# Fillers at TensorE's copy waits, and v and the state stored 64 columns wide, in a gated linear attention with a following feed-forward network

## The chip, the cores and the metric

The kernel runs on one core of a Trainium2 chip. A core has five engines that work side by side and each run their own queue of instructions in order: TensorE (PE, matmuls into PSUM), VectorE (DVE), ScalarE (ACT), GpSimd (POOL) and SyncE (SP, which here only issues the DMA transfers). They wait for one another through semaphores. The metric is the time of one execution on the device in microseconds (us); less is better.

## The reference, cut to what matters

The input is float32 for the attention and double precision for the four weights (the kernel reads the weights as pairs of 32-bit words). `B, H, S, D = 4, 8, 768, 48`; 3072 tokens; model width 384; inner width 1024.

```python
# attention: a complex decay per key channel, a state of D x D per head
scale = np.minimum(mag, 0.999) / (mag + 1e-06)          # mag = |a|
for t in range(S):
    S_re, S_im = ar * S_re - ai * S_im + kv, ar * S_im + ai * S_re   # kv = k_t outer v_t
    y[:, :, t] = q_t @ S_re
x = y.transpose(0, 2, 1, 3).reshape(B * S, H * D)
# feed-forward
a = x @ w1
b = x @ w2
return (a * b @ w3) @ w_out
```

## The kernel before

The time axis is cut into chunks of 128 steps. A *unit* is half a sequence of one batch, three chunks; there are eight units, and units 2n and 2n+1 share a state. Within a chunk the attention is a masked product: `scores` makes `A` = K'Q masked, `outputs` makes y from V and A and from the state T and Q, `turn` transposes the keys, `state` adds K'V to T. The gates (logarithms, exponentials, running products, sines) of the next unit are computed on ScalarE and VectorE while TensorE works on the present one. Each unit's FFN follows one unit behind. `w3` and `w_out` are multiplied together once at the start (`fuse`, the matmuls into `f`).

The order of TensorE's instructions is the order in which the program emits them (`manual_schedule`); a scheduler places the instructions of the other engines.

v is used where it lies, 48 columns per head. The matmuls of `outputs` take 32 columns of V at a time; the quadrants that lie across two heads need zeros beside the head's 16 columns, and only these are copied into the padded tile `V` (and `Tp` for the state):

```python
    def load_qkv(u):
        b, h = divmod(u, 2)
        if "q" not in g_t.get(u, {}):
            take_qk(u)
        g = g_t[u]
        load_rows(g["k"], kt, u)
        load_rows(g["q"], qt, u)
        g["vr"] = V_t[u] = two.tile([P, UC, DM], FP, tag="vr", name="vr")
        nc.sync.dma_start(out=g["vr"], in_=v[b, h * TT:(h + 1) * TT].rearrange("(c p) e -> p c e", p=C))

    def middle(X):
        return X.rearrange("p (h e) -> p h e", e=2 * D)[:, :, 32:64].rearrange("p h (two e) -> p h two e", two=2)

    def apart(X):
        return X.rearrange("p h two e -> p h (two e)")[:, :, 0:64].rearrange("p h (x e) -> p h x e", e=16)[:, :, 0::3]

    def spread_v(u):
        nc.scalar.copy(out=apart(Vb[u % 2].rearrange("p c h two e -> p (c h) two e")),
                       in_=middle(V_t[u].rearrange("p c e -> p (c e)")))

    def quadrant(X, Xp, q, i=0):

        return Xp[:, q // 3, i] if q % 3 == 1 else X[:, 32 * q:32 * q + 32]
# ... cut, from outputs:
        y = ps_v.tile([P, KD, C], FP, tag="v", name="y")
        lanes = [[] for _ in range(4)]
        for q in range(3 * H // 2):
            f, j = divmod(q, 4)
            o = y[32 * j:32 * j + 32, f]
            heads = [(q // 3 * 2 + (q % 3 + i) // 2, i) for i in range(2 if q % 3 == 1 else 1)]
            got = [(quadrant(V_t[u][:, c], Vb[u % 2][:, c], q, i), A[:, hd]) for hd, i in heads]
        # ... cut: the same with the state, then the matmuls, four lanes side by side
        with tc.high_priority():
            nc.scalar.copy(out=xT_t[u][:, :, w], in_=y)

    def state(u, c):

        KT, V = KT_t.pop((u, c)), V_t[u][:, c].rearrange("p (h e) -> p h e", h=H)
        n = u % 2 * UC + c
        T = T_t.get((u // 2, n))
        kv = ps_v.tile([2 * D, H, D], FP, tag="v", name="kv")
        for hd in range(H):
            nc.tensor.matmul(out=kv[:, hd], lhsT=KT[:, hd].rearrange("p d x f -> p (d x f)"), rhs=V[:, hd],
                             start=True, stop=True)
        Tn = three.tile([2 * D, H, D], FP, tag="T", name="T")
        Tp = Tb[(u // 2 * 2 * UC + n) % 3]
        new = middle(Tn.rearrange("p h e -> p (h e)"))
        with tc.high_priority():
            if T is None:
                nc.scalar.copy(out=Tn, in_=kv)
            else:
                nc.vector.tensor_tensor(out=Tn, in0=kv, in1=T[0], op=OP.add)
            if c == UC - 1:
                rho = L_t[u][1][:, :, TT:TT + 1].to_broadcast([2 * D, H, D])
                nc.vector.tensor_tensor(out=Tn, in0=Tn, in1=rho, op=OP.mult)
            nc.scalar.copy(out=apart(Tp), in_=new)
        T_t[u // 2, n + 1] = Tn, Tp
```

The feed-forward step of 128 inner columns, and the late checks (`look`: they read the gates and the weights again and sum up values out of bounds, for which a general version of the computation stands ready behind a branch):

```python
        a = two.tile([P, TT], FP, tag="a", name="a")
        with tc.high_priority():
            nc.scalar.copy(out=a, in_=got[0])
            nc.vector.tensor_tensor(out=ab_t[u][:, j], in0=got[1], in1=a, op=OP.mult)
# ... cut
    def check_weights(late):

        for u in range(2):
            for f in range(KD):
                re = late.tile([P, 2, TT], FP, tag="look", name="look")
                load_rows(re, art, u, [f])
                check_gates(u, re[:, 0], re[:, 1], f)
                yield
# ... cut, the weights' part:
                    raw = late.tile([P, 512, 2], I32, tag="look", name="look")
                    nc.sync.dma_start(out=raw[:, 0:step // 2].rearrange("p m w -> p (m w)"), in_=src[:, i, j:j + step])
                    lo, hi = (raw[:, 0:step // 2, x].bitcast(FP) for x in range(2))
                    nc.scalar.activation(out=hi, in_=hi, func=AF.Square, scale=2.0 ** 15)
                    nc.scalar.activation(out=lo, in_=hi, func=AF.Relu, scale=-1.0, bias=TINY, accum_out=st_wts[:, n:n + 1])
```

The order of unit 0 and of its FFN. `pieces(0)` holds ten groups (transposes, `kv`, `sc`, `y`); `fill` holds what is left of `fuse`, four entries of two matmuls each:

```python
        take_qk(1)
        rest = ffn(0, 2)
        work = work[2:]
        for i, p in enumerate(pieces(0)):
            for f in p:
                f()
            if i in (0, 1, 3, 5):
                fill.pop(0)()
            if i == 0:
                for f in work[:2]:
                    f()
                load_qkv(1)
            if i >= 2:
                next(steps)
            if i in (5, 7):
                work[2 + (i == 7)]()
        for i, f in enumerate(rest[:HEAD]):
            f()
            if i < 2:
                work[4 + i]()
            if i == 2:
                phase.close()
            if i < 6:
                next(steps)
        head_pool[1] = fast.enter_context(tc.tile_pool(name="late_heads", bufs=1))
        for _ in steps:
            pass
        load_gates(2)
```

For the later units, `unit` deals the parts of the FFN evenly over the pieces:

```python
    def ffn(u, parts=1):
        return [lambda j=j: ffn_ab(u, j) for j in range(KF)] + [p for t in range(UC) for p in ffn_out(u, t, parts)]

    def unit(u, steps, rest, look, ahead):

        for f in rest[:ahead]:
            f()
            next(steps, None)
        rest = rest[ahead:]
        p = pieces(u) + [[]]
        n = len(p)
        for i in range(n):
            for f in rest[i * len(rest) // n:(i + 1) * len(rest) // n] + p[i]:
                f()
                next(steps, None)
            next(look, None)
```

Of the kernel before, what the change touches and what calls it, by code (L numbers as in the profile page):

```python
# [10 lines left out]
FP = mybir.dt.float32  # L11
# [363 lines left out]
def kernel(  # L375
# [81 lines left out]
    Vb = [singles.tile([P, UC, H // 2, 2, 32], FP, name=f"V{i}") for i in range(2)]  # L457
    Tb = [singles.tile([2 * D, H // 2, 2, 32], FP, name=f"Tp{i}") for i in range(3)]
# [22 lines left out]
    g_t, L_t, xT_t, ab_t, T_t, KT_t, V_t = {}, {}, {}, {}, {}, {}, {}  # L481
# [18 lines left out]
# [4 lines that stand above are left out]
        g = g_t[u]  # L504
        load_rows(g["k"], kt, u)
        load_rows(g["q"], qt, u)
        g["vr"] = V_t[u] = two.tile([P, UC, DM], FP, tag="vr", name="vr")
        nc.sync.dma_start(out=g["vr"], in_=v[b, h * TT:(h + 1) * TT].rearrange("(c p) e -> p c e", p=C))

    def middle(X):
        return X.rearrange("p (h e) -> p h e", e=2 * D)[:, :, 32:64].rearrange("p h (two e) -> p h two e", two=2)

    def apart(X):
        return X.rearrange("p h two e -> p h (two e)")[:, :, 0:64].rearrange("p h (x e) -> p h x e", e=16)[:, :, 0::3]

    def spread_v(u):
        nc.scalar.copy(out=apart(Vb[u % 2].rearrange("p c h two e -> p (c h) two e")),
                       in_=middle(V_t[u].rearrange("p c e -> p (c e)")))  # L520

    def quadrant(X, Xp, q, i=0):

        return Xp[:, q // 3, i] if q % 3 == 1 else X[:, 32 * q:32 * q + 32]

    def check_gates(u, re, junk, f=0):
        for x, (scale, bias) in enumerate(((-1.0, LEAST), (1.0, MOST))):
            nc.scalar.activation(out=junk, in_=re, func=AF.Relu, scale=scale, bias=bias,
                                 accum_out=st_low[:, x, u, f:f + 1])
# [146 lines left out]

    def outputs(u, c):
        QL = L_t[u][0]
        w = slice(c * C, (c + 1) * C)
        A = Ab[(u * UC + c) % 2]  # L680
# [6 lines left out]
        for q in range(3 * H // 2):  # L687
            f, j = divmod(q, 4)
            o = y[32 * j:32 * j + 32, f]
            heads = [(q // 3 * 2 + (q % 3 + i) // 2, i) for i in range(2 if q % 3 == 1 else 1)]  # L690
            got = [(quadrant(V_t[u][:, c], Vb[u % 2][:, c], q, i), A[:, hd]) for hd, i in heads]
            if not first:
                got += [(quadrant(T[0].rearrange("p h e -> p (h e)"), T[1], q, i), QL[:, hd, w]) for hd, i in heads]
# [7 lines left out]
    def state(u, c):  # L701

        KT, V = KT_t.pop((u, c)), V_t[u][:, c].rearrange("p (h e) -> p h e", h=H)
        n = u % 2 * UC + c
        T = T_t.get((u // 2, n))
        kv = ps_v.tile([2 * D, H, D], FP, tag="v", name="kv")
# [3 lines left out]
        Tn = three.tile([2 * D, H, D], FP, tag="T", name="T")  # L710
        Tp = Tb[(u // 2 * 2 * UC + n) % 3]
        new = middle(Tn.rearrange("p h e -> p (h e)"))
        with tc.high_priority():
            if T is None:
                nc.scalar.copy(out=Tn, in_=kv)
            else:
                nc.vector.tensor_tensor(out=Tn, in0=kv, in1=T[0], op=OP.add)
            if c == UC - 1:
                rho = L_t[u][1][:, :, TT:TT + 1].to_broadcast([2 * D, H, D])
                nc.vector.tensor_tensor(out=Tn, in0=Tn, in1=rho, op=OP.mult)  # L720
            nc.scalar.copy(out=apart(Tp), in_=new)
        T_t[u // 2, n + 1] = Tn, Tp

    def ffn_ab(u, j):
# [10 lines left out]
        with tc.high_priority():  # L735
            nc.scalar.copy(out=a, in_=got[0])  # L736
# [57 lines left out]

    def check_weights(late):

        for u in range(2):
            for f in range(KD):
                re = late.tile([P, 2, TT], FP, tag="look", name="look")
                load_rows(re, art, u, [f])  # L800
                check_gates(u, re[:, 0], re[:, 1], f)
                yield
        n = 0
        for w in (w1, w2, w3t, wo):
# [4 lines left out]
            for i in range(src.shape[1]):  # L809
                for j in range(0, src.shape[2], step):  # L810
# [3 lines left out]
                    nc.scalar.activation(out=hi, in_=hi, func=AF.Square, scale=2.0 ** 15)  # L814
# [221 lines left out]
```

## Time and profile before

| | |
|---|---|
| time, median of 3 runs | 597.53 us (597.53 to 598.36) |
| span of the profiled execution | 596.5 us |
| mean TensorE clock granted | 0.982 of full speed |
| matmul records on TensorE | 3514 |
| DMA traffic | 84.71 MB, mean 142 GB/s |

How to read the lines that follow in this document. In the list of waits a line names the waiting engine with the instruction's output and line, then what released it, then us in total, times, and the longest. In a timeline a line gives start and duration in us, the engine, the line, the operation, output<-input, the shape, how many were merged, and in brackets the idle time ahead and what ended it. A group line ends with total busy us, the mean of one in ns, and idle time ahead. A float32 matmul makes two records. The span in 40 slices (the digit is tenths of the slice; PEclk is the granted clock):

```profile
PE   4669989999889999999799999999999999999996
DVE  5998399744851675159311685258413683300110
ACT  6897668548973798298622988398534652101100
PEclk9779999999899999999899999999999999999999
DMA  9777997295584658633932447815920007000001
```

After the fourth slice (one is 14.9 us) TensorE is busy nearly throughout. In the first four the weights are loaded and converted on ScalarE and VectorE, and TensorE waits for them.

### The profile page before, as it was taken

What the parts mean: (1) busy time and instruction counts of PE and PEld (TensorE: products, weight loads), DVE (VectorE), ACT (ScalarE), POOL (GpSimd) and SP (SyncE); (2) the same over time, 40 slices, a digit from 0 to 9 for tenths busy, and PEclk for the clock granted to TensorE, in tenths of its full rate; (3) what the DMA queues carried; (4) which work ended last, traced back from release to release, by engine and by line L of the source; (5) the groups of instructions that cost most, each with busy time, mean ns of one, the idle gap of its engine ahead of it and who ended that gap; (6) DMA issues with size and microseconds to landing.
All of it is one profiled execution on the core that took longest, in us unless ns stands there. A gap on an engine that the chain in (4) does not pass through costs nothing.

```text
span 596.5 us, 8841 instructions
## 1 busy us (share of the span) xinstructions
PE 556.7 (93%) x3514; PEld 366.5 (61%) x3514; DVE 302.0 (51%) x420; ACT 349.3 (59%) x584; POOL 5.1 (1%) x14
## 2 busy tenths in 40 slices
PE   4669989999889999999799999999999999999996
PEld 2335775567456766676366765776567656766553
DVE  5998399744851675159311685258413683300110
ACT  6897668548973798298622988398534652101100
POOL 3000000000000000000000000000000000000000
PEclk9779999999899999999899999999999999999999
DMA  9777997295584658633932447815920007000001
GB/s 289 277 282 227 262 333 204 80 233 154 159 221 114 178 174 207 161 118 105 233 86 67 126 157 188 225 54 154 246 78 1 14 32 154 1 14 29 1 1 44
DMA packets 46050, 84.71 MB, mean 142 GB/s; under 512 B 4656, under 2 KB 36144, under 8 KB 45104
## 3 DMA queue, kind: packets, MB, share of 16 engines
q1 hardware_dynamic: 46000, 84.06, 50.4%
q8 instruction: 29, 0.48, 0.4%
q14 instruction: 21, 0.17, 0.1%
HBM read 60.42 MB, written 4.72 MB: 109 GB/s over the span
## 4 chain that ended last, share of the span: by engine, by line
PE 56%; ACT 15%; DMA 13%; DVE 10%; issue 2%; SPq 2%; DVEq 0%; ACTq 0%
PE m L731 31%; PE o L747 13%; PE sc L672 4%; PE y L697 3%; PE kv L708 3%; DMA vr<-in_v_dram 3%; ACT gZ L552 3%; DMA im<-in_a_im_dram 2%; DMA look<-in_a_re_dram 2%; PE tp L660 2%; ACT re L552 2%; DMA raw<-in_w_dram 1%; ACT gA L552 1%; ACT look L815 1%; DVE gZ L608 1%
## 5 line engine op out<-in xcount | busy, mean ns | idle before, releaser
L731 PE MATMUL m<-xT,w1s 128*128 128x384 f32 x384 | 137.1, 494 | 4.0 <-ACT xT L699 3.7
L731 PE MATMUL m<-xT,w2s 128*128 128x384 f32 x384 | 136.0, 491 | 4.6 <-ACT ot L751 4.6
L747 PE MATMUL o<-w3o,ab 128*128 128x384 f32 x384 | 130.1, 492 | 0.0
L731 PEld LDWEIGHTS m<-xT,w2s 128*128 128x128 f32 x384 | 73.5, 192 | 57.1 <-ACT ot L751 5.9
L737 DVE TENSOR_TENSOR ab<-m,a 128x384 f32<-128x384 f32 x64 | 35.4, 555 | 141.6 <-PE m L731 127.6
L731 PEld LDWEIGHTS m<-xT,w1s 128*128 128x128 f32 x384 | 70.9, 192 | 48.7 <-ACT xT L699 5.8
L747 PEld LDWEIGHTS o<-w3o,ab 128*128 128x128 f32 x384 | 71.0, 190 | 48.5 <-issue 3.8
L736 ACT COPY a<-m 128x384 f32<-128x384 f32 x64 | 30.4, 475 | 64.0 <-PE m L731 64.0
L861 PE MATMUL f<-wo_s,w3s 128*128 128x384 f32 x128 | 48.8, 540 | 19.5 <-DVE wo_s L784 19.5
L662 ACT COPY KT<-tp 128x384 f32<-128x384 f32 x40 | 33.6, 846 | 42.0 <-PE tp L660 41.9
L861 PEld LDWEIGHTS f<-wo_s,w3s 128*128 128x128 f32 x128 | 26.6, 214 | 39.0 <-DVE wo_s L784 21.4
L672 PE MATMUL sc<-QL,KL 96*128 96x128 f32 x384 | 47.9, 278 | 2.0 <-DVE A L674 1.9
L672 PEld LDWEIGHTS sc<-QL,KL 96*128 96x128 f32 x384 | 45.6, 192 | 6.0 <-DVE A L674 3.3
L674 DVE COPY_PREDICATED A<-causal,sc 128x512 f32<-128x512 int32 x48 | 34.5, 739 | 13.4 <-PE sc L672 12.7
L697 PE MATMUL y<-A,vr 128*32 128x128 f32 x384 | 36.2, 277 | 0.0
L697 PE MATMUL y<-A,V 128*32 128x128 f32 x384 | 34.5, 274 | 0.0
L708 PEld LDWEIGHTS kv<-vr,KT 128*96 128x96 f32 x320 | 29.6, 165 | 3.2 <-ACT KT L662 1.1
L697 PE MATMUL y<-QL,T 96*32 96x128 f32 x320 | 31.5, 272 | 0.0
L708 PE MATMUL kv<-vr,KT 128*96 128x48 f32 x320 | 29.7, 246 | 0.7 <-ACT KT L662 0.7
L751 ACT COPY ot<-o 128x384 f32<-128x384 f32 x24 | 11.2, 467 | 32.4 <-PE o L747 32.4
L697 PE MATMUL y<-QL,Tp 96*32 96x128 f32 x320 | 29.8, 272 | 0.0
L697 PEld LDWEIGHTS y<-A,V 128*32 128x32 f32 x384 | 28.1, 109 | 0.0
(104 smaller groups left out, 664.0 us busy)
## 6 DMA issues: line engine op xcount, KB each, us to landing
look<-in_w_dram SPq DMA_DIRECT2D x28, 512.0 KB, 4.4
raw<-in_w_dram SPq DMA_DIRECT2D x7, 1024.0 KB, 8.4
raw<-in_w_dram SPq DMA_DIRECT2D x8, 768.0 KB, 6.4
KL<-gR SPq DMA_DIRECT2D x24, 192.5 KB, 3.5
KL<-k SPq DMA_DIRECT2D x24, 192.5 KB, 4.2
re<-in_a_re_dram SPq DMA_DIRECT2D x24, 192.0 KB, 5.9
im<-in_a_im_dram SPq DMA_DIRECT2D x24, 192.0 KB, 4.3
k<-in_k_dram SPq DMA_DIRECT2D x24, 192.0 KB, 3.5
```

Source lines behind the costliest of these rows:

```text
L552: chain(nc.scalar.activation(**kw))
L660: nc.tensor.transpose(out=tp[:, f], in_=src[:, f, c * C:(c + 1) * C], identity=ident)
L662: nc.scalar.copy(out=KT_t[u, c][:, :, :, x].rearrange("p h d f -> p f d h"), in_=tp.rearrange("p f (d h) -> p f d h", h=H))
L672: nc.tensor.matmul(out=sc[:, j], lhsT=KL[:, x * n + j, w], rhs=QL[:, x * n + j, w], start=True, stop=True)
L674: nc.vector.copy_predicated(out=A[:, x * n:(x + 1) * n], data=sc, mask=causal.rearrange("p (h t) -> p h t", h=1).to_broadcast([P, n, C]))
L697: nc.tensor.matmul(out=o, lhsT=a, rhs=b, start=s0, stop=s1)
L708: nc.tensor.matmul(out=kv[:, hd], lhsT=KT[:, hd].rearrange("p d x f -> p (d x f)"), rhs=V[:, hd], start=True, stop=True)
L731: nc.tensor.matmul(out=m, lhsT=w[:, j * P // WB, f, j * P % WB:j * P % WB + P], rhs=xT_t[u][:, f], start=(f == 0), stop=(f == KD - 1))
L736: nc.scalar.copy(out=a, in_=got[0])
L737: nc.vector.tensor_tensor(out=ab_t[u][:, j], in0=got[1], in1=a, op=OP.mult)
L747: nc.tensor.matmul(out=m, lhsT=ab_t[u][:, f, t * P:(t + 1) * P], rhs=w3o[:, f], start=(f == 0), stop=(f == KF - 1))
L861: nc.tensor.matmul(out=sums[j], lhsT=w3_t[f][:, j * P:(j + 1) * P], rhs=w3_t["wo"][:, f], start=(f == 0), stop=(f == KF - 1))
```

## The change

It has these parts:

- v and the state are stored 64 columns wide per head, 48 of them used, so that every quadrant has its zeros; `spread_v` copies all of v in two copies, `state` writes the wide T in one, and the copies `Tp` go. The tile `vr` has one buffer instead of two, and the `kv` matmuls read the wide V (64 columns moving instead of 48).
- Unit 0 and unit 1: the fillers (matmuls that wait for nothing) are emitted at other places between the attention's pieces, namely where it waits for a copy out of PSUM.
- The heads' tiles of unit 1 are allocated earlier and the last steps of its gates are emitted inside the FFN's loop, ahead of the stores.
- `follow`: a late check is ordered on ScalarE behind the last FFN copy `a` emitted so far.
- The first row of w3 is loaded and converted in four parts instead of two, and the tiles A are cleared on VectorE instead of GpSimd.

The diff, cut to its core:

```diff
-    Vb = [singles.tile([P, UC, H // 2, 2, 32], FP, name=f"V{i}") for i in range(2)]
-    Tb = [singles.tile([2 * D, H // 2, 2, 32], FP, name=f"Tp{i}") for i in range(3)]
+    Vb = [singles.tile([P, UC, H, 64], FP, name=f"V{i}") for i in range(2)]
...
 # load_qkv: vr
+        vr = one.tile([P, UC, DM], FP, tag="vr", name="vr")
+        nc.sync.dma_start(out=vr, in_=v[b, h * TT:(h + 1) * TT].rearrange("(c p) e -> p c e", p=C))
+        g["vr"] = vr
...
     def spread_v(u):
-        nc.scalar.copy(out=apart(Vb[u % 2].rearrange("p c h two e -> p (c h) two e")),
-                       in_=middle(V_t[u].rearrange("p c e -> p (c e)")))
-
-    def quadrant(X, Xp, q, i=0):
-
-        return Xp[:, q // 3, i] if q % 3 == 1 else X[:, 32 * q:32 * q + 32]
+        vr = g_t[u]["vr"].rearrange("p c (h two d) -> p c h two d", two=2, d=D)
+        V = Vb[u % 2].rearrange("p c (h two) e -> p c h two e", two=2)
+        for i, e0 in enumerate((0, 64 - D)):
+            nc.scalar.copy(out=V[:, :, :, i, e0:e0 + D], in_=vr[:, :, :, i])
...
-        KT, V = KT_t.pop((u, c)), V_t[u][:, c].rearrange("p (h e) -> p h e", h=H)
+        KT, V = KT_t.pop((u, c)), Vb[u % 2][:, c]
         n = u % 2 * UC + c
         T = T_t.get((u // 2, n))
-        kv = ps_v.tile([2 * D, H, D], FP, tag="v", name="kv")
+        kv = ps_v.tile([2 * D, H, 64], FP, tag="v", name="kv")
         for hd in range(H):
             nc.tensor.matmul(out=kv[:, hd], lhsT=KT[:, hd].rearrange("p d x f -> p (d x f)"), rhs=V[:, hd],
                              start=True, stop=True)
-        Tn = three.tile([2 * D, H, D], FP, tag="T", name="T")
-        Tp = Tb[(u // 2 * 2 * UC + n) % 3]
-        new = middle(Tn.rearrange("p h e -> p (h e)"))
+        Tn = three.tile([2 * D, H, 64], FP, tag="T", name="T")
         with tc.high_priority():
             if T is None:
                 nc.scalar.copy(out=Tn, in_=kv)
             else:
-                nc.vector.tensor_tensor(out=Tn, in0=kv, in1=T[0], op=OP.add)
-            if c == UC - 1:
-                rho = L_t[u][1][:, :, TT:TT + 1].to_broadcast([2 * D, H, D])
-                nc.vector.tensor_tensor(out=Tn, in0=Tn, in1=rho, op=OP.mult)
-            nc.scalar.copy(out=apart(Tp), in_=new)
-        T_t[u // 2, n + 1] = Tn, Tp
+                nc.vector.tensor_tensor(out=Tn, in0=kv, in1=T, op=OP.add)
+        if c == UC - 1:
+            rho = L_t[u][1][:, :, TT:TT + 1].to_broadcast([2 * D, H, 64])
+            nc.vector.tensor_tensor(out=Tn, in0=Tn, in1=rho, op=OP.mult)
+        T_t[u // 2, n + 1] = Tn
 
     def ffn_ab(u, j):
         if j == 0:
@@ -733,7 +724,7 @@
             got.append(m)
         a = two.tile([P, TT], FP, tag="a", name="a")
...
-            nc.scalar.copy(out=a, in_=got[0])
+            copied[:] = [nc.scalar.copy(out=a, in_=got[0])]
...
+    copied = []
+
+    def follow(work):
+
+        for ins in work:
+            tc.add_manual_dep(ins.ins, copied[-1].ins.name, ORDER, reason="later")
+
...
-                check_gates(u, re[:, 0], re[:, 1], f)
+                follow(check_gates(u, re[:, 0], re[:, 1], f))
...
-                    nc.scalar.activation(out=hi, in_=hi, func=AF.Square, scale=2.0 ** 15)
+                    follow([nc.scalar.activation(out=hi, in_=hi, func=AF.Square, scale=2.0 ** 15)])
...
-        nc.gpsimd.memset(A, 0.0)
-    for V in Vb + Tb:
+        nc.vector.memset(A, 0.0)
+    for V in Vb:
         nc.gpsimd.memset(V, 0.0)
 
...
+        first = [i * len(rest) // n for i in range(n + 1)] if u > 1 else [0, 1, 1, 2, 2, 3, 3, 3, 4, 4, 6]
         for i in range(n):
-            for f in rest[i * len(rest) // n:(i + 1) * len(rest) // n] + p[i]:
+            for f in rest[first[i]:first[i + 1]] + p[i]:
...
-        row_work(0, 2)
+        row_work(0, 4)
...
-            if i in (0, 1, 3, 5):
+            if i in (1, 3, 6, 9):
...
                 phase.close()
+                head_pool[1] = fast.enter_context(tc.tile_pool(name="late_heads", bufs=1))
             if i < 6:
                 next(steps)
-        head_pool[1] = fast.enter_context(tc.tile_pool(name="late_heads", bufs=1))
-        for _ in steps:
-            pass
-        load_gates(2)
+            if i == KF - 1:
+                for _ in steps:
+                    pass
+                load_gates(2)
         late = fast.enter_context(tc.tile_pool(name="late", bufs=2))
         look = check_weights(late)
         for u in range(1, NU):
```

## The prediction

> **What bounds the kernel now.** I read the page's busy shares first, then TensorE's waits, then its timeline for when each wait falls, then ScalarE's timeline for what ScalarE did at that moment. Busy shares, engine by engine:
>
> ```profile
> PE 556.7 (93%) x3514; PEld 366.5 (61%) x3514; DVE 302.0 (51%) x420; ACT 349.3 (59%) x584; POOL 5.1 (1%) x14
> ```
>
> TensorE (PE) is busy 556.7 of 596.5 us. A faster kernel must have fewer PE instructions or fewer of the remaining 39.8 us of holes. The waits of PE (us in total, times, longest):
>
> ```profile
> PE f L861 <- DVE wo_s L784: 19.5, 4, 8.3
> PE m L731 <- ACT ot L751: 4.6, 2, 3.8
> PE m L731 <- ACT xT L699: 3.7, 3, 2.6
> PE tp L660 <- DVE gR L624: 3.4, 2, 2.0
> PE sc L672 <- DVE A L674: 1.9, 2, 1.0
> PE kv L708 <- ACT KT L662: 0.7, 1, 0.7
> ```
>
> 19.5 us is the start, where the weights are converted. The other lines, with 0.2 us behind the copy `a`, are 14.5 us. What remains of the 39.8, some 5.6 us, is the tail after the last matmul. The timeline of PE places the waits (start, busy, instruction, idle before it in brackets):
>
> ```profile
> 86.05 2.20 PE L731 MATMUL m<-xT,w1s 128*128 128x384 f32 x6 [0.60 <-ACT xT L699]
> ...
> 118.75 0.52 PE L660 MATMUL tp<-ident,gR 128*128 128x128 f32 x3 [1.46 <-DVE gR L624]
> ...
> 154.77 3.86 PE L731 MATMUL m<-xT,w1s 128*128 128x384 f32 x6 [2.59 <-ACT xT L699]
> 170.29 0.52 PE L660 MATMUL tp<-ident,gR 128*128 128x128 f32 x3 [1.98 <-DVE gR L624]
> ...
> 295.10 3.67 PE L731 MATMUL m<-xT,w2s 128*128 128x384 f32 x6 [3.85 <-ACT ot L751]
> ```
>
> Two things matter. Up to 172 us the holes are in units 0 to 2; afterwards there is one large hole. And behind the two longest holes the same six matmul records take 3.86 and 3.67 us instead of 2.20: about 1.6 us each on top. So the removable cost after the start is 14.5 + 3.2 = 17.7 us, and 597.5 - 17.7 = 579.8 us is the floor for a change that leaves PE's work and the start alone.
>
> What ScalarE (ACT) did ahead of the 3.85 us hole:
>
> ```profile
> 287.36 1.28 ACT L556 ACT_TABLE_LOAD   x1
> 293.44 0.51 ACT L519 COPY V<-vr 128x384 f32<-128x384 f32 x1 [4.80 <-DMA vr<-in_v_dram]
> ...
> 294.59 0.46 ACT L751 COPY ot<-o 128x384 f32<-128x384 f32 x1
> ```
>
> The copy of v for a later unit stood in ACT's queue ahead of `ot`, and its load had not landed: it was issued at 283.69 us, with a load of `look` (late checks) immediately ahead, and landed 9.7 us later. Ahead of the 2.59 us hole ACT has no wait, only work: from 140 to 153 us it ran six `look` checks, two weight checks and the gates of unit 2 among the `xT` copies.
>
> [...] `ot` (needed) stands 4.80 us behind a V copy (not yet needed). [...] the trace has the slow batches of 3.86 and 3.67 us, already after 2.59 us idle, and none after 1.98. [...] 16 kv records follow each other in 1.32 us on the chain that ended last, 82.5 ns each. [...]
>
> **The change, part by part.**
>
> *v and state back to 64 columns per head.* PE's instruction count doesn't move: 16 products of V and 16 of T per chunk in both, and `kv` has the same 8 heads. Its moving side grows from 48 to 64 columns. I take that as free: records follow at 82.5 ns, [...] and an f32 record of 384 columns is spaced 322 ns (1.935 us for six), hence 0.84 ns per column and 54 ns for 64, still under 82.5. If wrong, it costs 16 x 0.84 ns x 320 records = 4.3 us. ACT loses the Tp copies and gains on V:
>
> ```profile
> L721 ACT COPY Tp<-T 96x128 f32<-96x128 f32 x20 | 6.0, 302 | 35.2 <-DVE T L717 21.4 <-DVE T L720 13.7
> ...
> L519 ACT COPY V<-vr 128x384 f32<-128x384 f32 x8 | 4.1, 508 | 7.1 <-DMA vr<-in_v_dram 7.1
> ```
>
> -6.0 us of Tp; V becomes 16 copies of 576 elements. Copies of 384 take 0.51 and ACT passes of 1152 take 1.16, so about 0.68 each, 10.9 in all, +6.8. ACT +0.8 us, DVE about +2.5 us on the 20 state writes (0.55 to 0.68): both beside PE. But `kv` now needs V, so the load of v and its spread move ahead of `kv`.
>
> *Fillers in unit 0.* The four pairs of `f` matmuls (1.3 us each) leave places 0, 1, 3, 5 for 1, 3, 6, 9. The last sits between the last `y` and the first `m`, where 0.60 us was lost; the third between two `sc` groups, where 0.97 was lost. Gain 1.6. In return the last `kv` follows its transposes with nothing between: a KT copy of 0.85 us, so I book 1.0 lost.
>
> *Fillers in unit 1.* Four `o` matmuls (2.6 us) come ahead of the first transpose, covering the 1.46 of gR; four more before the first `kv`, covering the 0.65; eight (5.2 us) between the last `y` and `m`, covering the 2.59 and so its 1.6 of slow clock. Sum 6.3. But only three groups of four now stand ahead of the first `sc` instead of also one after it: it wants QL and KL about 11.8 us after unit 0's FFN ends. Before, it came 12.8 us after the first transpose, with the moves landing just in time; I allow 1 us.
>
> *Checks behind the FFN copies.* In the changed queue of ACT no `look` stands between 100 us and unit 2's FFN. That frees about 7 us of ACT time from unit 2's gates. They wait also for VectorE and for their loads, so I take a gain of 3 to 5 us for gR of unit 2, ready at 165.6 instead of 170.2. PE, gaining its own holes, reaches that transpose at about 164 to 165.5. I therefore count all holes up to there together as 4.7 us gained, not as their full sum of 8.7 + 1.6 + 2.0.
>
> *v loads.* In the changed queue of SyncE, v of units 3, 4 and 5 are issued about one unit earlier. This removes the 3.85 and its 1.6 of slow clock: 5.4 us. The 0.6 at 285 us and the 0.8 at 423 us come from similar queues of ACT; I count 0.4 of the two.
>
> *Start.* The first row of w3 comes in quarters, with three raw buffers, so the loads of the gates are held behind the conversion; two memsets of A move to DVE, inside its first 3.37 us of idleness. Nearly the same bytes pass at some 265 to 280 GB/s, and DVE is busy 19.36 of 20 us afterwards. I book +0.5.
>
> *A new wait.* In ACT's queue one V copy of unit 1 now stands ahead of unit 0's last `xT`. Before, that load landed at 86.2 us, after the `xT` of 85.5. With one more load of k ahead it lands near 87, while PE would want `xT` at 85: up to 3.4 us, plus 1.6 of slow clock. It is absorbed by the unit-2 limit above, because gR of unit 2 and not PE's arrival sets that time.
>
> Sum: -4.7 - 5.4 - 0.4 + 0.5 = -10.0 us: 597.5 - 10.0 = 587.5 us.
>
> **Rivals.** (1) *All holes close.* For it: eight of the twelve holes have a filler or an earlier load right there. Against it: gR of unit 2 depends on a chain through ACT, DVE and loads that no filler shortens. It gives about 580. (2) *The V copies take over.* `kv` and `y` both hang on V, and V copies stand in ACT's queue ahead of `xT` and `ot`; with one vr buffer a late spread also delays the next load. For it: the only long hole after 172 us was exactly this, 4.80 us. Against it: v is issued earlier. With two holes of 4 us and their slow clock it gives 595 to 598. (3) *The wider kv costs its 4.3 us*: 592. Against it: the spacing of 82.5 ns.
>
> **Range and chances.** 580 (rival 1) to 597 (rival 2) holds nearly all I can name. 2% below is 585.6, only 1.9 us under my figure, so faster by over 2% gets 0.36. Slower by over 2% needs 12 us of new holes against 10 us of removed ones: 0.03.
>
> **What would show it.** Right: no PE wait behind `ot` near 290 us; a hole of 2 to 4 us before the first `m` of unit 0 with an ACT V copy waiting for vr; the first transpose of unit 2 near 166 us; kv records still about 82 ns apart. Wrong: the first `f` of the last row more than 2 us from where it is (59.65 us), a hole before `kv` behind V, or `look` waits ahead of `ot` in units 3 to 6.

## The result and the profile after

The changed kernel takes 588.39 us (median of 4 runs, 587.98 to 590.35), the kernel before, measured beside it, 597.81 us (4 runs, 597.53 to 598.36). The ratio is 0.9848, with a 95% interval of 0.9824 to 0.9872: 9.4 us or 1.5% faster. The span of the profiled execution went from 596.5 to 586.2 us.

Busy shares on the page of the changed kernel:

```profile
PE 552.6 (94%) x3514; PEld 365.7 (62%) x3514; DVE 306.6 (52%) x426; ACT 351.0 (60%) x576; POOL 3.5 (1%) x9
```

TensorE has the same 3514 matmul records. What went is idle time, 39.8 us before and 33.6 now, and 4.1 us of busy time; 3.1 of these are the two slow batches of the kernel before (3.86 and 3.67 against 2.20 us). VectorE has 4.6 us more work and ScalarE 1.7 more. The span fell by 10.3 us and the median by 9.4: the profile of the kernel before is of the longest of its runs, that of the changed kernel of the shortest. TensorE's waits in the changed kernel (us in total, times, longest):

```profile
PE f L859 <- DVE wo_s L775: 20.0, 4, 7.4
PE tp L652 <- DVE gR L616: 3.2, 1, 3.2
PE m L722 <- ACT xT L693: 1.5, 1, 1.5
PE sc L664 <- DVE A L666: 1.5, 4, 0.6
```

The line behind `ot`, 4.6 us before, is gone. The wait for gR is as large as before (3.2 against 3.4), but is one wait and not two. Where the waits lie, from TensorE's timeline (start, busy, instruction, idle before it):

```profile
60.44 2.85 PE L859 MATMUL f<-wo_s,w3s 128*128 128x384 f32 x8 [1.44 <-DVE wo_s L775]
71.91 1.57 PE L702 MATMUL kv<-V,KT 128*96 128x64 f32 x16 [0.92 <-ACT KT L654]
...
88.67 2.20 PE L722 MATMUL m<-xT,w1s 128*128 128x384 f32 x6 [1.51 <-ACT xT L693]
132.41 4.01 PE L664 MATMUL sc<-QL,KL 96*128 96x128 f32 x32 [0.79 <-issue]
167.13 0.52 PE L652 MATMUL tp<-ident,gR 128*128 128x128 f32 x3 [3.23 <-DVE gR L616]
...
194.84 2.05 PE L664 MATMUL sc<-QL,KL 96*128 96x128 f32 x16 [0.30 <-DVE A L666]
```

After 167 us only three waits of 0.30 us are left, this one and two more at the same place of units 4 and 6. They are a price of the wide state: ahead of that copy of A VectorE makes two state writes of 0.69 us, where the kernel before has two of 0.55 and no wait; every run with wide v shows these waits (0.29 to 0.32 us each), none with narrow v does. From the first `sc` to the first `y` it is 4.28 us (192.54 to 196.82) against 4.03 before (195.69 to 199.72), so some 0.25 us each.

Unit 2's first transpose stands at 167.13 us instead of 170.29. It divides the gain: 3.2 us before it and 7.1 us behind it (from there to the end of the span it was 426.2 us and is 419.1). ScalarE's timeline shows the two V copies that matter, of unit 1 and of unit 5:

```profile
87.57 0.67 ACT L516 COPY V<-vr 128x576 f32<-128x576 f32 x1 [3.11 <-DMA vr<-in_v_dram]
88.15 0.47 ACT L693 COPY xT<-y 128x384 f32<-128x384 f32 x1
...
288.70 1.25 ACT L516 COPY V<-vr 128x576 f32<-128x576 f32 x2
```

At 87.57 a V copy waits 3.11 us for its load and holds the `xT` behind it: that is TensorE's hole of 1.51 us. At 288.70, where 4.80 us were lost before, nothing waits: the load was issued at 224.26 us, where it was 283.69. In the kernel before, the last `y` matmul of unit 3 still reads the buffer that this load needs until 279.04 us; in the changed kernel the buffer is free when unit 4's V copies are done (222.31 us).

### The profile page after: what moved, and what is told of

The parts are those of the page before. It is cut to its first block, busy times and chain, and to the rows that moved or that the text cites. A ratio compares the mean times of both kernels' runs of the same rounds, so it can differ in the third digit from the quotient of the medians.

```text
span 586.2 us, 8856 instructions
## 1 busy us (share of the span) xinstructions
PE 552.6 (94%) x3514; PEld 365.7 (62%) x3514; DVE 306.6 (52%) x426; ACT 351.0 (60%) x576; POOL 3.5 (1%) x9
## 4 chain that ended last, share of the span: by engine, by line
PE 72%; DMA 9%; DVE 8%; ACT 6%; issue 2%; SPq 2%; ACTq 0%; DVEq 0%
PE m L722 34%; PE o L738 19%; PE y L691 5%; DMA raw<-in_w_dram 5%; PE sc L664 5%; PE kv L702 4%; DMA vr<-in_v_dram 3%; PE f L859 2%; PE tp L652 2%; ACT re L544 1%; SPq L485 1%; DMA re<-in_a_re_dram 1%; DVE gZ L600 1%; ACT low L764 1%; ACT low L766 1%
## 5 line engine op out<-in xcount | busy, mean ns | idle before, releaser
L722 PE MATMUL m<-xT,w1s 128*128 128x384 f32 x384 | 134.9, 488 | 1.5 <-ACT xT L693 1.5
L722 PE MATMUL m<-xT,w2s 128*128 128x384 f32 x384 | 134.4, 486 | 0.0
L691 PE MATMUL y<-A,V 128*32 128x128 f32 x768 | 39.3, 275 | 0.1
L691 PEld LDWEIGHTS y<-A,V 128*32 128x32 f32 x768 | 32.9, 109 | 5.5 <-issue 2.0
L691 PE MATMUL y<-QL,T 96*32 96x128 f32 x640 | 34.6, 272 | 0.0
L702 PEld LDWEIGHTS kv<-V,KT 128*96 128x96 f32 x320 | 29.6, 165 | 3.2 <-ACT KT L654 1.2
L691 PEld LDWEIGHTS y<-QL,T 96*32 96x32 f32 x640 | 31.3, 110 | 0.0
L702 PE MATMUL kv<-V,KT 128*96 128x64 f32 x320 | 30.0, 246 | 0.9 <-ACT KT L654 0.9
L544 ACT ACTIVATE re<-gZ 128x1152 int32<-128x1152 f32 (+3 forms) x20 | 19.2, 969 | 18.3 <-DVE gZ L600 14.6
(98 smaller groups left out, 586.2 us busy)
```

What stands on the lines that cost most here:

```text
L544: chain(nc.scalar.activation(**kw))
L691: nc.tensor.matmul(out=o, lhsT=a, rhs=b, start=s0, stop=s1)
L722: nc.tensor.matmul(out=m, lhsT=w[:, j * P // WB, f, j * P % WB:j * P % WB + P], rhs=xT_t[u][:, f], start=(f == 0), stop=(f == KD - 1))
```

## The experiments

In this program the order of TensorE's queue is written down; that of the other engines is chosen when the program is built, so a small edit can move other instructions too. Each run therefore says what stood where. Two distances turned out to carry the argument: from the start of unit 1's gR (VectorE; the keys times a part of the gates, which the transposes read) to unit 2's first transpose (TensorE), called the gate stretch, and from there to the end, called the rest. Both come from the one execution that was profiled, the median from all; executions of one kernel differ by up to 6.7 us (the kernel before, 593.68 to 600.42 beside e1 to e4). *Moves* are the DMA transfers into KL and QL, which `sc` reads; a *slow batch* is a group of matmuls behind a hole that takes about 1.4 to 1.8 us more than elsewhere (last section). All times in us; "ratio" is to runs of the kernel before made beside each run (medians 597.16 to 597.81), with its 95% interval.

| run | v, state | checks ordered | fillers, start | unit 1 gR | gate stretch | rest | median | ratio |
|---|---|---|---|---|---|---|---|---|
| before | narrow | no | old | 117.24 | 53.05 | 426.2 | 597.81 | 1 |
| after | wide | yes | new | 118.14 | 48.99 | 419.1 | 588.39 | 0.9848 [0.9824, 0.9872] |
| e1_no_follow | wide | no | new | 119.73 | 53.17 | 422.6 | 597.04 | 0.9997 [0.997, 1.0025] |
| e2_all_but_v | narrow | yes | new | 117.40 | 49.01 | 424.6 | 595.43 | 0.9966 [0.9936, 0.9996] |
| e3_old_fillers | wide | yes | old fillers | 117.29 | 48.56 | 419.0 | 588.53 | 0.9876 [0.9819, 0.9933] |
| e4_old_start | wide | yes | old start | 120.14 | 48.92 | 419.2 | 590.14 | 0.9896 [0.9834, 0.9957] |
| e5_follow_only | narrow | yes | old | 116.79 | 48.57 | 424.6 | 591.88 | 0.9906 [0.988, 0.9932] |
| e6_wide_v_only | wide | no | old | 119.75 | 49.83 | 421.0 | 591.40 | 0.9888 [0.9859, 0.9916] |
| e7_v_and_follow | wide | yes | old | 118.14 | 48.68 | 419.0 | 588.09 | 0.9847 [0.9827, 0.9867] |
| e9_v_on_gpsimd | narrow, copied by GpSimd | no | old | 116.87 | 53.26 | 421.0 | 593.05 | 0.9926 [0.9896, 0.9956] |

The gate stretch can be taken apart further. In every run of the table ScalarE begins unit 2's first gate instruction, gA, 16.4 to 16.6 us after unit 1's gR, so the difference lies behind it, from gA to unit 2's gR. The two ends, for the kernel before (first two lines) and the changed one:

```profile
133.74 1.17 ACT L552 ACTIVATE gA<-re 128x1152 f32<-128x1152 f32 x1 [1.12 <-DMA re<-in_a_re_dram]
168.78 1.36 DVE L624 TENSOR_TENSOR gR<-k,re 128x1152 f32<-128x1152 f32 x1 [2.46 <-ACT re L552]
...
134.65 1.17 ACT L544 ACTIVATE gA<-re 128x1152 f32<-128x1152 f32 x1 [6.05 <-DMA re<-in_a_re_dram]
165.62 1.36 DVE L616 TENSOR_TENSOR gR<-k,re 128x1152 f32<-128x1152 f32 x1 [0.60 <-ACT re L544]
```

That is 35.0 us before and 31.0 after. Without the ordering it is 35.0 to 35.3 (before, e1, e9), with it 30.6 to 31.0; e6, at 31.7, is the exception that the argument has to explain.

The theory to be tested was that of the prediction (T, later T2): the late load of v made the long hole, the checks made unit 2's gates late, and the gates, not TensorE's arrival, set unit 2's first transpose. The rivals: the ordering of the checks did it all, or the fillers did.

**e1_no_follow: the changed kernel without the ordering of the checks.**

```
-                follow(check_gates(u, re[:, 0], re[:, 1], f))
+                check_gates(u, re[:, 0], re[:, 1], f)
...
-                    follow([nc.scalar.activation(out=hi, in_=hi, func=AF.Square, scale=2.0 ** 15)])
+                    nc.scalar.activation(out=hi, in_=hi, func=AF.Square, scale=2.0 ** 15)
```

> The changed kernel without its ordering of the late checks behind the FFN copies. In its queue of ScalarE the two copies of v of unit 5 stand ahead of `ot` again, as in the kernel before, and look checks stand among unit 2's gates again; its v loads keep the changed kernel's early place in SyncE's queue. Theory T (that of the prediction: the long hole near 290 us was a late v load, and the change removed it by an earlier load): no TensorE hole over 1 us between 280 and 300 us although the V copies stand ahead of `ot`; only unit 2's gates are later, so its first transpose is at 169 to 171 instead of 167.1; 590.5 to 592.5 us in all. Rival R1 (the ordering removed it): a hole of 3 to 4 us and a slow batch behind it near 290 us, on top of the later gates; 595 to 598 us. Rival R2 (the fillers carry the gain, the ordering is worth nothing): 588 to 589 us.

Measured: 597.04 us; the whole gain is gone, more than theory T allowed. The long hole did not come back: one V copy stands right ahead of `ot` at 293.49 us and one behind it at 294.43, neither waits, and the largest hole between 280 and 300 us is 0.79. So R1 falls as far as that hole goes. The loss lies in the gate stretch, 53.17 instead of 48.99, and in what follows the longer wait. TensorE's timeline of this run:

```profile
172.90 0.87 PE L652 MATMUL tp<-ident,gR 128*128 128x128 f32 x3 [5.84 <-DVE gR L616]
173.56 3.52 PE L722 MATMUL m<-xT,w1s 128*128 128x384 f32 x6
```

The wait for gR is 5.84 us, not 3.23, and the nine records behind it take 1.8 us more than usual (0.87 and 3.52 against 0.52 and 2.10). Two more holes, 0.79 and 0.55 us, came later. The 9.3 us between the two spans are 1.6 of a later gR of unit 1, 4.2 of the gate stretch and 3.5 of the rest. ScalarE spent 12.9 us on `look` checks between the two gR's (12.3 in the kernel before, none in the changed one).

**e2_all_but_v: the kernel before with everything but the wide v and state** (fillers, start, heads and ordering as in the change's diff; `spread_v`, `outputs` and `state` as before).

> The kernel before with every part of the change but the wide v and state: fillers, order of checks, start, loads of unit 2's gates. v stays as it is where it needs no spreading, so its buffer is freed only by the last product that reads it. Theory T: up to the first transpose of unit 2 as in the changed kernel (near 167 us, 3.2 us gained). The v load of unit 5 is late again (issued after 270 us), its copy stands in ScalarE's queue a little later, behind the first FFN copy, and the wait moves to what follows it, the KT copies: a hole of 2 to 4 us near 290 to 300 us; 592 to 595 us. Rival R1 (the ordering of the checks removed the long hole): no such hole, 588 to 589.5 us. Rival R2 (the fillers carry all of it): 588 to 589.5 us too.

Measured: 595.43 us in the median, 0.4 above theory T's range; the profiled execution took 592.83 us (span 591.0), so the profile shows where things stood but not all of the median. Gate stretch 49.01 and first transpose at 166.41: as theory T said. The load of v of unit 5 was late again, issued at 280.65 us. But no hole of 2 to 4 us followed near 290: in ScalarE's queue the V copy now stood behind unit 4's first FFN copy, at 293.21, and by then the load was there. Theory T missed here: the ordering of the checks removes the long hole too, in its own way. In its place a hole of 2.47 us opened at 228.46 behind `a`. R1 had said that no long hole would follow, and none did; but R1 and R2 wanted the whole gain here, and fall.

**e3_old_fillers: the changed kernel with the fillers where they were.**

```
-        first = [i * len(rest) // n for i in range(n + 1)] if u > 1 else [0, 1, 1, 2, 2, 3, 3, 3, 4, 4, 6]
+        first = [i * len(rest) // n for i in range(n + 1)]
...
-            if i in (1, 3, 6, 9):
+            if i in (0, 1, 3, 5):
```

> The changed kernel with the fillers of units 0 and 1 back in their old places. Theory T (the gate chain of unit 2 and not TensorE's arrival sets its first transpose, which waits 3.2 us in the changed kernel): the old holes of 0.6, 1.0, 1.5 and 0.7 us come back before it, 3.7 us or a little more, of which the 3.2 us wait absorbs most; first transpose of unit 2 at 167 to 169 us, 588.5 to 590.5 us in all. Rival R2 (the fillers carry the gain): all the holes they covered come back in full, with the slow batch before the first `m` of unit 1, 594 to 597 us.

Measured: 588.53 us, the same as with the fillers. The holes came back (0.59, 0.88, 0.70, 0.88 and 1.99 us), and TensorE reached unit 2's first transpose at 165.85 us (earlier than the 167 to 169 of theory T, for unit 1's gR was 0.85 us earlier), just as gR was done, with no wait. The two are tied: the hole of 1.99 us is a wait for an `xT` that stood in ScalarE's queue behind unit 2's gates (a table load at 152.31, `xT` at 153.61), so the gates hold TensorE here too, only earlier; e5 and e7 have the same hole (1.98 and 1.48 us) and no wait for gR either. The fillers buy time that is then waited away; R2 falls.

**e4_old_start: the changed kernel with the old start.**

```
-        row_work(0, 4)
+        row_work(0, 2)
...
-        nc.vector.memset(A, 0.0)
+        nc.gpsimd.memset(A, 0.0)
```

> The changed kernel with the first row of w3 in halves again and the two memsets of A on GpSimd. In the kernel before the last `f` of the first run began at 59.65 us, in the changed one at 60.44. Theory T: the start is worth 0.5 to 0.8 us, but unit 2's gate chain hangs on loads and moves that hang on the start as well, so what is gained stays: 587.5 to 588.2 us. Rival R3 (the change of the start was itself a gain that other terms hid): 589.5 us or more. Rival R4 (the start is wholly absorbed by the wait before unit 2): 588.4 us, with that wait 0.8 us longer.

Measured: 590.14 us, with an interval that overlaps the changed kernel's. The last row of `f` began at 58.33 us, 2.1 earlier. The gain did not last: the first `sc` of unit 0 then waited 1.94 us, and its sixteen matmuls took 3.75 us instead of 2.05. The profile names the load of re as what ended the wait; it was issued at 66.81, right behind the last of unit 0's moves (66.10), which `sc` needs.

```profile
73.31 3.75 PE L664 MATMUL sc<-QL,KL 96*128 96x128 f32 x16 [1.94 <-DMA re<-in_a_re_dram]
```

Unit 1's gR came at 120.14, the latest in the table. The median points towards R3, but run e7, with the old start and the old fillers, is at 588.09; what the start is worth by itself is not settled.

**e5_follow_only and e6_wide_v_only: the kernel before with one of the two parts; e7_v_and_follow: with both**, and with the old fillers, start and heads. e5 adds to the kernel before only:

```
+    copied = []
+    def follow(work):
+        for ins in work:
+            tc.add_manual_dep(ins.ins, copied[-1].ins.name, ORDER, reason="later")
...
-            nc.scalar.copy(out=a, in_=got[0])
+            copied[:] = [nc.scalar.copy(out=a, in_=got[0])]
...
-                check_gates(u, re[:, 0], re[:, 1], f)
+                follow(check_gates(u, re[:, 0], re[:, 1], f))
```

(and the same `follow` around the Square of the weight checks; `check_gates` now returns its instructions). e6 has the hunks of `Vb`, `load_qkv`, `spread_v`, `outputs` and `state` from the change's diff and nothing else; e7 has both.

> The kernel before with one part of the change alone: the late checks ordered behind the FFN copies. Numbers so far: from the start of unit 1's gR to the start of unit 2's gR, both on VectorE, it is 51.5 us in the kernel before, 51.7 in the changed kernel without the ordering, and 47.0 to 47.5 in the three runs with it. Theory T2 (the ordering is what shortens the gate chain, and the chain and not the fillers sets unit 2's first transpose): the stretch is 47 to 48 us here too, with the first transpose of unit 2 at 166 to 167.5 us instead of 170.3; afterwards some 1.6 us are gained as in the run with all but the wide v, whose long hole near 290 us went and one of 2.5 us came near 228 us; 591 to 593.5 us in all. Rival R5 (the ordering does nothing without fillers): stretch near 51.5, 596 to 598 us. Rival R6 (the ordering carries everything): 588 to 589.5 us.

> The kernel before with the other part alone: v and state at 64 columns. Theory T2: the gate chain stays at 51 to 52 us and the first transpose of unit 2 at 170 to 172 us; the v load of unit 5 is issued near 225 us instead of 284 and the long hole near 290 us is under 1 us; some 3.6 us gained after unit 2's first transpose, 593 to 595 us in all. Rival R5 (wide v gains nothing without the ordering): 596 to 598 us. Rival R6 (wide v carries everything): 588 to 589.5 us.

> The kernel before with wide v and with the ordering of the checks, but with the old fillers, the old start and the old place of unit 2's gate loads. Theory T2 (these two parts are the whole gain; fillers and start are worth nothing where the gate chain sets the end): chain 47 to 48 us, first transpose of unit 2 at 165.5 to 167 us, no hole over 1 us afterwards, 587 to 589.5 us as in the changed kernel. Rival R2 (the fillers or the start are needed): 591 us or more.

Measured: 591.88, 591.40 and 588.09 us. e5 and e7 fall where T2 put their times; e6 gained 1.6 us more than it allowed, and T2 missed there in the mechanism too: from gR to gR it had asked for 51 to 52 us, and it was 48.3. e5: gate stretch 48.57, first transpose at 165.36 (0.6 earlier than T2 said), and later the hole behind `a` that e2 had too:

```profile
225.82 3.04 PE L731 MATMUL m<-xT,w2s 128*128 128x384 f32 x6 [2.54 <-ACT a L736]
```

e6: the load of v of unit 5 is issued at 219.65, the largest hole between 280 and 300 us is 0.80, and the rest is 421.0 instead of 426.2: 5.2 us from v alone. Its gate stretch is 49.83, though 11.0 us of checks still run on ScalarE between the two gR's (but unit 1's gR is 2.5 us later than before, so its first transpose, at 169.58, is only 0.7 us earlier). Where e1 loses more than e6 can be read off: from gA to the instruction that makes gZ from gA it is 11.5 us in e1, 12.0 in the kernel before, 9.7 in e6 and 9.5 in the changed kernel. In e1 a check stands right ahead of it and waits for its own load (in the kernel before too, 1.01 us); in e6 it waits for VectorE alone. ScalarE in e1, then in e6:

```profile
147.16 0.62 ACT L519 ACTIVATE look<-look,consts 128x384 f32<-128x384 f32 x1 [1.07 <-DMA look<-in_a_re_dram]
...
146.01 1.26 ACT L544 ACTIVATE gZ<-gA,consts 128x1152 f32<-128x1152 f32 x1 [0.47 <-DVE gA L567]
```

So the traces speak for the place of the checks in the queue rather than their amount; moving single checks was not tried. e7 is the result that settles the accounts: two parts give the whole gain, and fillers, start and early heads add nothing to it.

**e9_v_on_gpsimd: the kernel before with its eight V copies on GpSimd.**

```
-        nc.scalar.copy(out=apart(Vb[u % 2].rearrange("p c h two e -> p (c h) two e")),
+        nc.gpsimd.tensor_copy(out=apart(Vb[u % 2].rearrange("p c h two e -> p (c h) two e")),
```

> The kernel before with the eight copies of v moved from ScalarE to GpSimd; the loads of v stay as late as they were and the late checks as they were. Theory T2 (the 3.85 us hole near 295 us and its slow batch exist because a V copy that waits for its load stands in ScalarE's queue ahead of `ot`): the load of v of unit 5 is still issued after 275 us, but there is no hole over 1 us near 295 us; the gate chain of unit 2 stays at 50 to 52 us; 591 to 593 us in all. Rival R9 (the late load itself or the bandwidth it shares makes the hole, whoever copies): a hole of 2 us or more behind `y` or `m` between 285 and 340 us, 595 to 598 us.

Measured: 593.05 us, at the edge of what T2 said. The load of unit 5 is late (285.37 us) and GpSimd waits for it, but `ot` doesn't. GpSimd's timeline and then ScalarE's:

```profile
292.52 0.97 POOL L519 COPY V<-vr 128x384 f32<-128x384 f32 x1 [68.07 <-DMA vr<-in_v_dram]
```

```profile
291.05 0.48 ACT L751 COPY ot<-o 128x384 f32<-128x384 f32 x1
```

After 171 us TensorE has one hole left, 0.69 us. The late load was harmless here, where nothing urgent stood behind the copy that waited 68.07 us on GpSimd; R9 falls. The gate stretch stayed at 53.26.

**e10_v_load_first: the changed kernel with v loaded ahead of k and q.**

```
-        load_rows(g["k"], kt, u)
-        load_rows(g["q"], qt, u)
         vr = one.tile([P, UC, DM], FP, tag="vr", name="vr")
...
+        load_rows(g["k"], kt, u)
+        load_rows(g["q"], qt, u)
```

> The changed kernel with v loaded ahead of k and q of the same unit, not behind them. Theory T2 (the 1.5 us wait of the first `m` of unit 0 for a V copy is absorbed by the later wait for unit 2's gR): v of unit 1 lands some 4 us earlier, the hole of 1.5 us falls below 0.7, the wait ahead of unit 2's first transpose grows to 4 to 4.7 us, and the whole stays at 587.5 to 589 us. Rival R10 (TensorE's holes add up): 586 to 587 us.

Measured: 590.52 us, ratio 0.9867 [0.9826, 0.9908]. v of unit 1 was issued at 74.19 instead of 78.28, and the hole of 1.51 us ahead of the first `m` went. Nothing was gained by it, against R10; but the test is not clean, for the edit moved v of unit 0 as well, and the last row of `f` now waited 2.79 us with a slow batch behind it. Unit 1's gR was 1.3 us later, the gate stretch was 49.09, and the wait ahead of unit 2's first transpose 3.23 as before, not longer.

**e8_re_early, e11_re_between_moves and e12_re_between_v_first: three attempts to take the wait of 3.23 us away.** In the changed kernel unit 2's first gate load (re) is issued at 127.41, behind twelve moves, and ScalarE begins gA at 134.65, after 6.05 us of waiting for it; e8 issues it ahead of the moves, e11 between KL's and QL's, e12 as e11 with v loaded first. All give one filler group more ahead of unit 1's first `sc`; e8 delays the gates of unit 2 in ScalarE's queue, e11 and e12 tie those on VectorE to the copies of A.

```
             if i == KF - 1:
+                load_gates(2, ("re",))          # e8; in e11 and e12 ahead of move(QL, ...) of unit 1
                 for _ in steps:
                     pass
-                load_gates(2)
+                load_gates(2, ("im",))
...
-        ... else [0, 1, 1, 2, 2, 3, 3, 3, 4, 4, 6]
+        ... else [0, 1, 1, 2, 2, 3, 4, 4, 4, 4, 6]
...
+                if u > 1 or waited[u] > 7:      # unit 2's gates begin seven pieces later
                     next(steps, None)
```

> The changed kernel with the first gate load of unit 2 (re) issued ahead of unit 1's twelve moves instead of behind them, the gates of unit 2 kept behind unit 1's copies in ScalarE's queue, and one group of four `o` matmuls moved ahead of unit 1's first `sc`, to cover moves that start 1.9 us later. Theory T2 (the 3.2 us that TensorE waits for unit 2's gR hang on that load, issued at 127.4 and landed at 134.6 us): re lands at 126 to 130 us, gR of unit 2 comes 3 to 6 us sooner, the wait ahead of unit 2's first transpose falls below 1 us, and 585 to 586.5 us in all. Rival R7 (the chain hangs on ScalarE's and VectorE's work or on the other loads of unit 2, not on re): the wait stays over 2 us, 587.5 to 590 us. Rival R8 (the later moves or later copies of xT open a hole as long): no gain, with a hole of 2 to 4 us ahead of `sc` or `m` of unit 1.

> The last run's idea repaired. The changed kernel with unit 2's load of re issued between unit 1's moves of KL and those of QL, one group of four `o` matmuls ahead of unit 1's first `sc`, and unit 2's gates on VectorE kept behind unit 1's masked copies of A, so that these no longer stand behind the gate chain. Theory T2: re is issued at 123 to 125 us instead of 127.4 and lands near 131; from unit 1's gR to unit 2's gR it is 43 to 45 us instead of 47.5; the wait ahead of unit 2's first transpose falls below 1.5 us; 585 to 587 us in all. Rival R7 (the chain hangs on other work, re is not what it waits for): the stretch stays near 47 us, 588 to 590 us. Rival R8 (copies or moves of unit 1 come later and open a hole of 2 us or more ahead of `sc` or `y`): 588 us or more.

> The run before with v loaded ahead of k and q as well. Theory T2: once gR of unit 2 no longer sets the time, TensorE's own holes count, so the 1.5 us hole that goes is now worth up to its length: 0.5 to 1.5 us under the run before, 584 to 586 us. Rival R10 (the holes before unit 2 stay absorbed): no difference to the run before.

Measured: 609.67 [ratio 1.0186, 1.0156 to 1.0217], 592.21 [0.9923, 0.9894 to 0.9951] and 590.54 us [0.9886, 0.9847 to 0.9925]. In e11 it was as R8 said. In e8 the hole stood ahead of `sc`, where R8 looked for one, but it was 15.60 us long and had another cause. e12 was 1.7 us under e11, with intervals that overlap, and has the same hole (4.49 us), so that what it was to tell apart, whether TensorE's own holes count once the gates come sooner, stays open. In e8 the masked copies of A stand behind unit 2's gates in VectorE's queue; VectorE's and TensorE's timelines:

```profile
158.39 1.36 DVE L596 TENSOR_TENSOR k<-k,gR 128x1152 f32<-128x1152 f32 x1
159.67 1.32 DVE L673 COPY_PREDICATED A<-causal,sc 128x512 f32<-128x512 int32 x2
```

```profile
160.44 3.78 PE L671 MATMUL sc<-QL,KL 96*128 96x128 f32 x16 [15.60 <-DVE A L673]
```

The scores were finished at about 145 us, their copies began at 159.67. In e11 the first two copies of A still stood behind two gate instructions, and gA of unit 2 behind an `ot` that waited for the filler I had moved:

```profile
135.67 0.48 ACT L758 COPY ot<-o 128x384 f32<-128x384 f32 x1 [5.70 <-PE o L754]
136.04 1.17 ACT L548 ACTIVATE gA<-re 128x1152 f32<-128x1152 f32 x1
```

```profile
143.12 3.78 PE L680 MATMUL sc<-QL,KL 96*128 96x128 f32 x16 [4.57 <-DVE A L682]
```

re was issued at 124.85 there, 2.6 us earlier, and gA ran at 136.04, 1.4 us later than in the changed kernel, as was unit 1's gR (119.49 against 118.14). That re is what unit 2's gates wait for stays supported by the traces that show that wait only (6.05 us in the changed kernel); no run here profited from an earlier re, and none is faster than the changed kernel.

## Why the prediction was right, point by point

**Total.** Predicted 587.5 us, measured 588.39. Two errors of about 1 us went against each other: the part up to unit 2's first transpose was to give 4.2 us with the start counted in and gave 3.2; the part behind it was to give 5.8 and gave 7.1. That the total came out closer than its parts is luck. The "full sum of 8.7 + 1.6 + 2.0" that the prediction sets aside is too large as well: the six holes ahead of the wait for gR (0.97, 0.60, 1.46, 0.65, 0.92 and 2.59) are 7.2 us; nothing hangs on it.

**The long hole (-5.4).** Right in mechanism: e9 shows that the V copy in ScalarE's queue made it, and e6 that the wide v, which frees its load's buffer at the copy, brings the load forward and takes 5.2 us off the rest. Incomplete in cause: the prediction gave it to the v loads alone, and in e2 and e5 the ordering of the checks removed it with the load still late. Either part alone removes it; the changed kernel has both. The size was short because a hole ahead of `m` costs more than its idle time. In the kernel before, four holes of 5.43 us in all stood behind 172 us. The six records behind each take 2.20 us where six in a stream take 1.93, 0.27 more, so 1.1 us for four; the slow batch adds 1.47. That is 8.0 us; the changed kernel has three waits of 0.30 in their place, which leaves 7.1. The prediction had booked 0.4 of the 1.58 us of short holes and nothing for the 0.27.

**Unit 2's gates (-4.7).** The step that set the time was named rightly: the gate chain and not TensorE. TensorE arrived at 163.90 us ("about 164 to 165.5"). The term was mis-sized: "ready at 165.6 instead of 170.2" is 4.6 us, and gR was ready at 166.98 (165.62 and its 1.36 us) instead of 170.14, 3.2 us. That gR began at 165.62 is a coincidence of numbers. The gain "of 3 to 5 us" by the ordering was right for the stretch, which is 4.1 us shorter and 48.6 to 49.0 us in every run with the ordering in the table; but it began 0.9 us later, with unit 1's gR, and that was not booked. The ScalarE time freed was 12.3 us and not "about 7"; it gave 4.1.

**Fillers.** That their 7.9 us (1.6 and 6.3) do not add up was right, and the runs say more than the prediction did: they add nothing (e3, e7). The new holes booked were of the right kind: `kv` 0.92 (1.0 booked), `sc` of unit 1 0.79 (1.0), the V copy ahead of the first `m` of unit 0 1.51 (up to 3.4), without a slow batch, and short of the "2 to 4 us" that the prediction gave as a sign.

**Start (+0.5).** 0.8 us in the profile of the changed kernel. In the six profiles with the new start and v loaded behind k and q (after, e1, e2, e3, e8, e11) the last row of `f` begins at 61.2 us on average (59.5 to 63.6), in the six with the old start at 59.1 (58.3 to 59.7), so the term is nearer 2.2; but as e4 shows, what is earlier there can be waited away a few microseconds later.

**kv free.** Right. In a stream of the changed kernel:

```profile
191.21 1.49 PE L702 MATMUL kv<-V,KT 128*96 128x64 f32 x16
192.54 2.00 PE L664 MATMUL sc<-QL,KL 96*128 96x128 f32 x16
```

From the first of the 16 records to what follows them it is 1.33 us, 83 ns each; with 48 columns it was 1.32 at the same place (194.37 to 195.69). One record takes 246 ns in the mean in both, and the rest of e7 is 7.2 us shorter with the same 320 records. VectorE's and ScalarE's extra work was larger than booked (4.6 and 1.7 us, booked 2.5 and 0.8). The prediction put it all beside TensorE's path; VectorE's part was not quite off it, for the two wider state writes are what the three waits of 0.30 us come from. Rival 3 is out; so is rival 2, for no V copy makes a hole after 100 us; rival 1 kept its 3.2 us from the gate chain.

**Left open.** Without the ordering, fillers, start and heads cost 5.6 us (e1 against e6), and without the wide v 3.5 us (e2 against e5); with both parts there they cost nothing. In e1 the place is the gate stretch, 3.3 us longer than in e6 with much the same check time on ScalarE (12.9 and 11.0 us); that those checks hurt and e6's hardly do because of their places in the queue is read from the traces and not shown by a run.

## What to carry to other kernels

Look for instructions in a queue that wait for something late and have something urgent behind them (in the kernel before a V copy waited 4.80 us on ScalarE, with `ot` behind it): taking the wait away (e6), moving the copy to another engine (e9), or ordering the less urgent work behind the urgent (e5) were each worth 4 to 6 us here. Before filling holes, find the chain that the filled time runs into; with the gate stretch at 48.6 to 49.0 us whatever the fillers did, all that they saved was waited away. And when a load is brought forward in a program whose queues are ordered for you, read the queues again: an earlier re put the gates ahead of the masked copies and cost 21 us.

## What the runs showed of the hardware that was not expected

The same wait is not always followed by slow records. In the changed kernel the wait of 3.23 us is followed by records of the usual length; in e10 a wait of 3.23 us at the same place is followed by six that take 3.79 us:

```profile
167.13 0.52 PE L652 MATMUL tp<-ident,gR 128*128 128x128 f32 x3 [3.23 <-DVE gR L616]
167.49 2.10 PE L722 MATMUL m<-xT,w1s 128*128 128x384 f32 x6
```

```profile
168.52 0.52 PE L650 MATMUL tp<-ident,gR 128*128 128x128 f32 x3 [3.23 <-DVE gR L614]
168.88 3.79 PE L720 MATMUL m<-xT,w1s 128*128 128x384 f32 x6
```

In the kernel before the slow records ran at a lower granted clock: it was 0.50 over the first 3.2 and 2.9 us of its two slow batches (154.77 to 158.00 and 295.10 to 298.00 us); in the changed kernel it was 1.00 over all of 160 to 172 us, the wait of 3.23 us included. Slow batches came after a wait of 1.94 us in e4 (3.75 us for the sixteen `sc` records instead of 2.05; mean granted clock 0.91 over 62 to 100 us) and of 2.54 us in e5 (3.04 and 3.00 us for twice six records instead of 2.10; 0.97 over 172 to 230 us). In e1 the clock was 0.96 over 100 to 140 us, where TensorE was idle for 1.77 us in all. No slow batch came after 1.98 us in the kernel before (1.00 over 170.29 to 172.60 us) or after 2.47 us in e2 (1.00 over 172 to 230 and 230 to 282 us). Why equal waits end differently is not shown by these runs. So in this kernel a hole of some 1.9 to 4 us is to be booked with a possible extra of 1.4 to 1.8 us (an estimate from the batches above and in the table's runs), not a certain one.
